# Running most of the first feed-forward's second product on scaled float16 halves

## The chip, the cores and the metric

One core of one Trainium2 chip runs the whole program. The metric is the device time of one launch in microseconds. The engines are named as the profile names them: PE (TensorE matmul), PEld (its weight loads), DVE (VectorE), ACT (ScalarE), POOL (GpSimd), SP (the queue that issues the DMAs).

## What is computed

Attention with a decay over 4 batches of 8 heads, 576 positions and a head size of 64, then two feed-forward layers over the 2304 tokens, with a model width of 512 and a hidden width of 2048.

```python
scores = scale * np.matmul(q, k.transpose(0, 1, 3, 2))
decay = cum[:, :, :, None] - cum[:, :, None, :]        # cum: running sum of log f
scores = np.where(causal, -1000000000.0, scores + decay)
attn = np.exp(scores - np.max(scores, axis=-1, keepdims=True))
attn = attn / (np.sum(attn, axis=-1, keepdims=True) + 1e-09)
x = np.matmul(attn, v)          # as 2304 x 512
h = x @ moe_w_in;   x = (h * (1.0 / (1.0 + np.exp(-h)))) @ moe_w_out
h = x @ moe2_w_in;  x = (h * np.cos(h)) @ moe2_w_out
```

All inputs are float32. A product of two matrices is made of three matmuls on two-part operands: high times high, high times low, low times high.

## The kernel before

The tokens are cut into 9 blocks of 256 (`NB`, `TB`), the hidden width into 8 pairs of 128-column chunks (`NPR`). A *step* is one layer, one block, one pair; `order` lists 72 steps of the first layer and 72 of the second. In a step the PE first makes `in` (L1086): two chunks times 4 pieces of the model width times 3 products, 24 matmuls of 128x128 by 128x256 on float16 halves, into a PSUM tile `h`. ACT and DVE then make the gated value: tanh (L1111, ACT), `d1` (L1114, DVE), `g` (copied to the high part by `copies`, L286 on ACT or L288 on DVE) and `gl` (the low part, by `rest`, L306 on DVE). Two steps later (`LAG`) the PE makes `out` (L1186 in the first layer): 24 matmuls of 128x128 by 128x256 that sum into the PSUM tiles `y` over the 8 pairs of a block. In the first layer `g` and `wo` are pairs of float32 words in the PE's rounded form (`F32R`); in the second layer (`strassen`, L989) both are float16 halves, 21 matmuls a step, and the weights come from DRAM, where the first layer's time is used to park them split (tile `w16`, store L863, load L1068).

Attention runs as 32 jobs, 16 of kind "a" and 16 of kind "b", whose units make `S` matmuls, maximum and exponential (L649 on DVE, L669 on ACT), transposes `T` (L686) and `pv` (L766). The output of attention goes to DRAM in `x_d`, is loaded as `x32`, and `split_tasks` makes the scaled float16 halves `x` of a block.

Nothing runs in the order of the code. Each piece of work is a `Task` with an engine, an estimated duration, a key, the tasks that it needs and the buffers that it takes; `Scheduler.run` plays them against its estimates, gives each free engine the ready task with the smallest key, and so writes one fixed instruction order per engine. An engine then executes its row in that order and waits where something is late. Some tasks may go to either of two engines.

```python
k_in, k_out, k_el = MK + n, MK + n + LAG[l] + 0.5, MK + n      # MK = -1000, n the step
ts = add("PE", pe, f_s, split + [masked], key=i - 10000.0, ...  # attention's S: ahead of all steps
t = add("PE", 0.1, f_sum, [t], key=key - 10000.0, acq=["s"], name="sc")   # a norm
```

So on the PE attention goes first where it is ready, and steps fill the rest; on ACT and DVE the elementwise work of the steps goes first, then attention by its position (0 to 152), then the second layer's weights (`C2K0` = 150 and up).

`scale_tasks` gives a power of two for a pair of operands: ACT squares them (L311), DVE adds (L376), the PE sums over the partitions with one matmul of one column (L380, "norm"), and DVE makes scale and inverse in four small steps (L385 to L388).

Of the kernel before, what the change touches and what calls it, by code (L numbers as in the profile page):

```python
# [23 lines left out]
TB = 256  # L24
# [19 lines left out]
W2N0, W2N1 = 16, 1.4  # L44
QA, QB = 768, 1600
# [223 lines left out]
def decay_attention_silu_cos_kernel(ctx, tc, qa, qb, f, w1i, w1o, w2i, w2o, out):  # L269
# [10 lines left out]
    w2_d = {("i", c): dr.tile([128, 2, 512], F16, name=f"w2i_d{c}") for c in range(NF)}  # L280
    w2_d.update({("o", p, k): dr.tile([128, 2, 512 if k < 3 else 256], F16, name=f"w2o_d{p}_{k}") for p in range(NPR)
# [33 lines left out]
    def sbt(tag, shape, dt=F32, name=None):  # L315
        return sb.tile(shape, dt, tag=tag, bufs=TOK[tag], name=name or tag)
# [19 lines left out]
    rg2 = sb.tile([128, NPR], F32, name="rg2")  # L336
    v2 = sb.tile([128, 2, NPR], F32, name="v2")
    vm = sb.tile([128, 4], F32, name="vm")
    ry2 = sb.tile([128, NB], F32, name="ry2")
# [28 lines left out]
    SW = lambda l, kind, p: 2 * NB + (0 if l == 1 else NPR if kind == "i" else 2 * NPR) + p  # L368
# [459 lines left out]

    w2_done = {}
# [72 lines left out]
    xready, factor, last_out = {}, {}, {}  # L902
# [32 lines left out]
    def factor_tasks(l, j, ts, key):  # L935
        k, o = SX(l, j), SW(l, "i", 0)

        def f1(p0, p1):
            def f():
                nc.vector.tensor_scalar(rg1[:, j, p0:p1], inv[:, o + p0:o + p1], inv[:, k:k + 1], 0.5, ALU.mult, ALU.mult)  # L940
            return f

        def f2():
            nc.vector.tensor_scalar(ru2[:, 0, j], inv[:, o:o + NPR], inv[:, k:k + 1], 1.0, ALU.mult, ALU.mult)
            nc.vector.tensor_scalar(ru2[:, 1, j], scl[:, o:o + NPR], scl[:, k:k + 1], 2.0 ** 100, ALU.mult, ALU.min)
            nc.vector.tensor_scalar(ru2[:, 1, j], ru2[:, 1, j], RND, None, ALU.mult)
            nc.vector.tensor_scalar(ry2[:, j:j + 1], inv[:, k:k + 1], vm[:, 1:2], 2.0 ** 16, ALU.mult, ALU.mult)
        if l == 2:
            t = add("DVE", 0.4, f2, [ts, factors2], key=key, name="sc")
            return [t] * NPR  # L950
        wts = [wready[1, "i", 2 * p][0] for p in range(NPR)]
        if j < 2:
            return [add("DVE", 0.1, f1(p, p + 1), [ts, wts[p]], key=key, name="sc") for p in range(NPR)]
        t = add("DVE", 0.1, f1(0, NPR), [ts] + wts, key=key, name="sc")
        return [t] * NPR
# [88 lines left out]
    for l, j, p in order:  # L1044
# [59 lines left out]
        if l == 1:  # L1104
# [11 lines left out]
            def half(i, s=(l, j, p)):  # L1116
                if s not in g_t:
                    g_t[s] = sbt("g", [128, 2, 2 * TB], F32R)
                return g_t[s][:, i]

# [3 lines left out]
            t3 = add(**copies(lambda half=half: half(0), src, 512, ("ACT", "DVE"), half_r), deps=[t2], key=k_el, acq=["g"],  # L1124
                     name="g")
            t4 = add(**rest(lambda half=half: half(1), src, half_r, lambda half=half: half(0).bitcast(F32), 512),
# [44 lines left out]
        prev = None  # L1171
        wdeps = [t for i in range(2) for t in wready[l, "o", 2 * p + i]]
        ytag = "s" if (l, j) == (1, 1) else "y"
        for t in range(2):
            for i in range(2):
# [23 lines left out]
                prev = add("PE", c_pe(1536, TB), f, [prev] if prev else [t3, t4, last_out.get((l, j))] + wdeps, key=k_out, acq=acq, rel=rel, name="out")  # L1199
        last_out[l, j] = prev  # L1200
        if p == NPR - 1:
            x2done.setdefault(j, [])
            for t in range(2):
                def ev(l=l, j=j, t=t, cell=cell):
                    cell["o", t] = sbt("s2", [128, 512], name="yo")
                    nc.scalar.activation(cell["o", t], y_t[l, j][t], AF.Copy)
# [3 lines left out]
                t0 = add("ACT", 0.49, ev, [prev], key=k_el, acq=["s2"], rel=[ytag], name="ev")  # L1210
# [51 lines left out]
```

## Time and profile before

| | us |
|---|---|
| median of 3 runs (982.35 to 983.75) | 983.35 |
| the profiled execution's own time | 983.18 |
| its span, first to last instruction | 981.3 |
| PE busy in the span | 955.5 |
| PEld busy | 826.4 |
| DVE busy | 757.2 |
| ACT busy | 628.0 |
| POOL busy | 123.2 |

The span is what the trace holds; 1.9 us of the profiled execution lie around it. Busy time of an engine is the time in which at least one of its instructions runs. Instructions overlap on an engine, so the length of one is more than its share of the busy time, and matmul ends are modelled: what a stream of matmuls costs is read from the starts of the groups. The timeline gives groups in order of time: start, length, engine, line, operation, operands and count, and in brackets the idle time before it.

### The profile page before, as it was taken

What the parts mean: (1) busy time and instruction counts of PE and PEld (TensorE: products, weight loads), DVE (VectorE), ACT (ScalarE), POOL (GpSimd) and SP (SyncE); (2) the same over time, 40 slices, a digit from 0 to 9 for tenths busy, and PEclk for the clock granted to TensorE, in tenths of its full rate; (3) what the DMA queues carried; (4) which work ended last, traced back from release to release, by engine and by line L of the source; (5) the groups of instructions that cost most, each with busy time, mean ns of one, the idle gap of its engine ahead of it and who ended that gap; (6) DMA issues with size and microseconds to landing.
All of it is one profiled execution on the core that took longest, in us unless ns stands there. A gap on an engine that the chain in (4) does not pass through costs nothing.

```text
span 981.3 us, 20944 instructions
## 1 busy us (share of the span) xinstructions
PE 955.5 (97%) x8223; PEld 826.4 (84%) x8223; DVE 757.2 (77%) x1792; ACT 628.0 (64%) x1219; POOL 123.2 (13%) x157
## 2 busy tenths in 40 slices
PE   7996899999999999999999999999999999999997
PEld 4475688887888878889999999988888888888886
DVE  4999976677879888858778742678888888878875
ACT  6896866577776768745455432676766766766663
POOL 4865320011111121200000000000000000000000
PEclk9998899999999999999999999999999999999999
DMA  8575234435566575334433338500010001000000
GB/s 305 182 267 195 92 108 154 157 118 177 174 208 186 181 224 189 102 115 146 167 125 125 108 128 255 193 23 23 23 44 23 23 23 44 1 23 1 23 22 22
DMA packets 55906, 115.27 MB, mean 117 GB/s; under 512 B 8128, under 2 KB 18368, under 8 KB 55808
## 3 DMA queue, kind: packets, MB, share of 16 engines
q1 hardware_dynamic: 55808, 113.94, 35.0%
q8 instruction: 64, 1.05, 0.4%
q14 instruction: 34, 0.28, 0.1%
HBM read 89.20 MB, written 24.72 MB: 116 GB/s over the span
## 4 chain that ended last, share of the span: by engine, by line
PE 89%; DVE 7%; issue 1%; ACT 1%; POOL 1%; POOLq 0%; DVEq 0%; ACTq 0%
PE h L1086 37%; PE y L1186 20%; PE y L989 17%; PE pv L766 4%; PE tt L686 4%; PE st L645 3%; DVE rw L438 2%; DVE w L442 1%; DVE wi L306 1%; PE st L638 1%; PE dp L584 1%; PE st L624 1%; PE st L623 1%; DVE e L649 1%; DVE wo L300 1%
## 5 line engine op out<-in xcount | busy, mean ns | idle before, releaser
L1086 PE MATMUL h<-x,wi 128*128 128x256 f16 x3456 | 412.2, 274 | 3.1 <-ACT wi L286 1.7
L1086 PEld LDWEIGHTS <-wi 128*128 128x128 f16 x3456 | 330.0, 98 | 52.7 <-issue 6.1
L1186 PE MATMUL y<-g,wo 128*128 128x256 f32 x1728 | 238.2, 290 | 4.4 <-ACT g L286 3.6
L1186 PEld LDWEIGHTS y<-g,wo 128*128 128x128 f32 x1728 | 216.4, 192 | 11.9 <-issue 6.1
L989 PE MATMUL y<-wo,g 128*128 128x256 f16 x1512 | 176.3, 273 | 0.0
L989 PEld LDWEIGHTS <-g 128*128 128x128 f16 x1512 | 148.0, 98 | 17.1
L669 ACT ACTIVATE e<-e,su 128x128 f32<-128x128 f32 (+4 forms) x144 | 82.9, 577 | 22.5 <-DVE su L649 20.8
L1135 ACT ACTIVATE t<-h,ru 128x512 f32<-128x512 f32 x72 | 49.4, 686 | 67.3 <-PE h L1086 67.1
L1111 ACT ACTIVATE t<-h,rg 128x512 f32<-128x512 f32 x72 | 49.3, 685 | 64.1 <-PE h L1086 62.7
L1158 DVE TENSOR_TENSOR g<-t,g 128x896 f16<-128x896 f32 x72 | 78.4, 1089 | 8.7 <-ACT g L1155 5.2
L649 DVE CUSTOM_DVE_ANT_0 e<-st,dk 128x256 f32<-128x256 f32 (+3 forms) x144 | 64.1, 478 | 23.8 <-PE st L645 13.4
L288 POOL TENSOR_SCALAR e<-e,su 128x128 f32<-128x128 f32 (+4 forms) x68 | 50.7, 751 | 247.5 <-DVE su L676 135.4
L1145 DVE SCALAR_TENSOR_TENSOR t<-h,rg,t 128x512 f32<-128x512 f32 x72 | 53.9, 749 | 31.8 <-ACT t L1142 31.8
L306 DVE SCALAR_TENSOR_TENSOR g<-t,rg,g 128x512 fp32r<-128x512 f32 x72 | 55.3, 769 | 28.8 <-ACT g L286 28.2
L1141 ACT ACTIVATE t<-t,ru 128x512 f32<-128x512 f32 x72 | 51.7, 718 | 39.9 <-DVE t L1138 39.9
L1114 DVE SCALAR_TENSOR_TENSOR t<-t,h 128x512 f32<-128x512 f32 x72 | 49.2, 683 | 35.0 <-ACT t L1111 34.5
L1155 ACT ACTIVATE g<-t 128x896 f16<-128x896 f32 x72 | 67.5, 938 | 5.0 <-DVE t L1151 5.0
L286 ACT ACTIVATE g<-t,rg 128x512 fp32r<-128x512 f32 x49 | 35.3, 721 | 53.3 <-PE y L1186 50.0
L1138 DVE SCALAR_TENSOR_TENSOR t<-t,ru,h 128x512 f32<-128x512 f32 x72 | 53.5, 743 | 20.4 <-ACT t L1135 19.9
L286 ACT ACTIVATE pt<-tt 128x384 f32<-128x384 f32 (+2 forms) x90 | 44.5, 518 | 23.5 <-PE tt L686 23.1
L686 PE MATMUL tt<-ident,e 128*128 128x128 f32 x384 | 55.7, 275 | 3.4 <-POOL e L288 2.8
L1142 ACT ACTIVATE t<-t,halfpi 128x512 f32<-128x512 f32 x72 | 52.0, 722 | 2.3
(128 smaller groups left out, 1146.7 us busy)
## 6 DMA issues: line engine op xcount, KB each, us to landing
rw<-w1i SPq DMA_DIRECT2D x16, 512.0 KB, 5.2
rw<-w1o SPq DMA_DIRECT2D x16, 512.0 KB, 6.8
x<-x_d SPq DMA_DIRECT2D x16, 512.0 KB, 3.9
dk<-decay_d SPq DMA_DIRECT2D x16, 512.0 KB, 4.2
raw<-w2i SPq DMA_DIRECT2D x16, 512.0 KB, 4.9
raw<-w2o SPq DMA_DIRECT2D x16, 512.0 KB, 4.4
qs<-qb SPq DMA_DIRECT2D x16, 480.0 KB, 4.6
w2o_d<-w SPq DMA_DIRECT2D x24, 256.0 KB, 2.1
```

What stands on the lines that cost most here:

```text
L286: nc.scalar.activation(dst, src, AF.Copy, scale=scale)
L306: fn=lambda: nc.vector.scalar_tensor_tensor(out(), a(), scale(), b(), ALU.mult, ALU.subtract))
L649: nc.vector.tensor_tensor_reduce(out, s, d, -0.125, first, ALU.add, ALU.min, cell["sm"][:, o:o + 1])
L669: nc.scalar.activation(x, x, AF.Exp, bias=sm[:, i:i + 1], scale=-1.0, accum_out=sm[:, 4 + i:5 + i])
L686: nc.tensor.transpose(tt[a][:, 128 * c:128 * c + 128], e[a][:, 128 * c:128 * c + 128], ident)
L989: nc.tensor.matmul(y[bank][:, 256 * half:256 * half + 256], g[:, gi, ga], w[:, wi, 256 * col:256 * col + 256], start=p == 0 and half == 0 ...
L1086: nc.tensor.matmul(h[:, i], w[:, wi, 128 * k:128 * k + 128], x[:, xi, k], start=(i == 0 and q == 0 and k == 0), stop=(i == 1 and q == 2 an ...
L1138: nc.vector.scalar_tensor_tensor(cell["t"], cell["t"], r, cell["h"], ALU.subtract, ALU.subtract)
L1145: nc.vector.scalar_tensor_tensor(cell["t"], cell["h"], r, cell["t"], ALU.mult, ALU.mult)
L1155: nc.scalar.activation(g_t[s][:, 0], cell["w"], AF.Copy)
L1158: nc.vector.tensor_tensor(g_t[s][:, 1], cell["w"], g_t[s][:, 0], ALU.subtract)
L1186: nc.tensor.matmul(y[:, e * TB:(e + 1) * TB], w[:, wi, 128 * ec:128 * ec + 128], g[:, gi, i * TB:(i + 1) * TB], start=(st and e == 0), sto ...
```

## The change

From the fourth block on (`J16` = 3, 48 of the 72 steps of the first layer) `out` multiplies float16 halves. For that the second weight matrix, which is there as two float32 parts in `wo`, is split once more: per pair a scale (`scale_tasks`, 8 of them, two squares each on ACT), per chunk the high half (`chi`, ACT or DVE), the remainder of the high part (`left`, DVE) and the low half (`low`, DVE), in a buffer `w16` of which there are two; the chunk is stored in DRAM (16 stores). When the third block has used a pair for the last time, its two chunks are loaded over the float32 parts, in the same place (16 loads). `g` and `gl` are written as float16 with a factor `rg3` that all pairs share, for which all eight scales must be there; the result is scaled back where `y` is read out (`ev`, ACT). The new weight work has keys 80 to 87, ahead of the second layer's weights and of the last jobs of attention.

```diff
+J16, C16 = 3, 80.0
...
+    w1_d = {c: dr.tile([128, 2, 512], F16, name=f"w1o_d{c}") for c in range(NF)}
...
-    SW = lambda l, kind, p: 2 * NB + (0 if l == 1 else NPR if kind == "i" else 2 * NPR) + p
+    SW = lambda l, kind, p: 2 * NB + NPR * (2 * l - 2 + (kind == "o")) + p
...
+    w1_done, sc1 = {}, []
+    for p in range(NPR):
+        k, key = SW(1, "o", p), C16 + p
+        pair = (2 * p, 2 * p + 1)
+        hi, lo = [lambda c, i=i: wo_t[c][:, i].bitcast(F32) for i in range(2)]
+        q = [add(**squares(lambda c=c, hi=hi: hi(c), 512, sq[:, c % 2, k:k + 1]), deps=wready[1, "o", c], key=key, name="sqw")
+             for c in pair]
+        ts = scale_tasks(k, q, key, 14)
+        sc1.append(ts)
+        for c in pair:
+            st = {}
+
+            def dst(i, st=st):
+                if "t" not in st:
+                    st["t"] = sbt("w16", [128, 2, 512], F16)
+                return st["t"][:, i]
+
+            def left(st=st, c=c, k=k, hi=hi):
+                st["w"] = sbt("s2", [128, 512], name="w")
+                nc.vector.scalar_tensor_tensor(st["w"], hi(c), scl[:, k:k + 1], st["t"][:, 0], ALU.mult, ALU.subtract)
+
+            def low(st=st, c=c, k=k, lo=lo):
+                nc.vector.scalar_tensor_tensor(st["t"][:, 1], lo(c), scl[:, k:k + 1], st["w"], ALU.mult, ALU.add)
+            t5 = add(**copies(lambda dst=dst: dst(0), lambda c=c, hi=hi: hi(c), 512, ("ACT", "DVE"), lambda k=k: scl[:, k:k + 1]),
+                     deps=[ts], key=key, acq=["w16"], name="chi")
+            t6 = add("DVE", c_dve(512), left, [t5], key=key, acq=["s2"], name="clo")
+            t6 = add("DVE", c_dve(512), low, [t6], key=key, rel=["s2"], name="clo")
+            w1_done[c] = add("SP", 0.46, lambda st=st, c=c: nc.sync.dma_start(w1_d[c], st["t"]), [t6], key=key, rel=["w16"],
+                             dma=c_dma(0.26), name="w2d")
+
+    def f_v1():
+        i, o = SW(1, "i", 0), SW(1, "o", 0)
+        nc.vector.tensor_tensor(v1[:, 0], scl[:, i:i + NPR], scl[:, o:o + NPR], ALU.mult)
+        nc.vector.tensor_tensor(v1[:, 1], inv[:, i:i + NPR], inv[:, o:o + NPR], ALU.mult)
+        nc.vector.tensor_reduce(vm[:, 2:3], v1[:, 0], AX.X, ALU.min)
+        nc.vector.tensor_reduce(vm[:, 3:4], v1[:, 1], AX.X, ALU.max)
+        nc.vector.tensor_scalar(rg3, v1[:, 1], vm[:, 2:3], 2.0 ** -16, ALU.mult, ALU.mult)
+    factors1 = add("DVE", 0.9, f_v1, sc1 + [wready[1, "i", 2 * p][0] for p in range(NPR)], key=-500, name="sc")
...
+        def f3():
+            nc.vector.tensor_scalar(ry1[:, j:j + 1], inv[:, k:k + 1], vm[:, 3:4], 2.0 ** 15, ALU.mult, ALU.mult)
+        if j >= J16:
+            ry_done[j] = add("DVE", 0.2, f3, [ts, factors1], key=key, name="sc")
...
                 if s not in g_t:
-                    g_t[s] = sbt("g", [128, 2, 2 * TB], F32R)
+                    g_t[s] = (sbt("g", [128, 2, 2 * TB], F32R) if s[1] < J16 else
+                              sbt("g", [128, 2, 4 * TB], F16)[:, :, 0:2 * TB])
                 return g_t[s][:, i]
+
+            def out_r(j=j, p=p, half_r=half_r):
+                return half_r() if j < J16 else rg3[:, p:p + 1]
+
+            def whole(j=j, half=half):
+                return half(0).bitcast(F32) if j < J16 else half(0)
 
             t1 = add("ACT", 0.49, a1, [prev, factor[l, j][p]], key=k_el, acq=["t"], name="tanh")
             t2 = add("DVE", 0.61, d1, [t1], key=k_el, rel=["h"], name="d1")
             src = lambda cell=cell: cell["t"]
-            t3 = add(**copies(lambda half=half: half(0), src, 512, ("ACT", "DVE"), half_r), deps=[t2], key=k_el, acq=["g"],
+            t3 = add(**copies(lambda half=half: half(0), src, 512, ("ACT", "DVE"), out_r),
+                     deps=[t2, factors1 if j >= J16 else None], key=k_el, acq=["g"],
                      name="g")
-            t4 = add(**rest(lambda half=half: half(1), src, half_r, lambda half=half: half(0).bitcast(F32), 512),
+            t4 = add(**rest(lambda half=half: half(1), src, out_r, whole, 512),
                      deps=[t3], key=k_el, rel=["t"], name="gl")
...
+        if j == J16:
+            for c in (2 * p, 2 * p + 1):
+                def load16(c=c):
+                    wo_t[c] = sb.tile([128, 2, 1024], F16, tag=f"wo{c}", bufs=1, name="wo")[:, :, 0:512]
+                    nc.sync.dma_start(wo_t[c], w1_d[c])
+                wready[1, "o", c] = [add("SP", 0.46, load16, [w1_done[c], out_done[J16 - 1, p]], key=k_in - 2, dma=c_dma(0.26),
+                                         name="w2l")]
...
-                prev = add("PE", c_pe(1536, TB), f, [prev] if prev else [t3, t4, last_out.get((l, j))] + wdeps, key=k_out, acq=acq, rel=rel, name="out")
-        last_out[l, j] = prev
+                prev = add("PE", (c_pe if j < J16 else c_pe16)(1536, TB), f, [prev] if prev else [t3, t4, last_out.get((l, j))] + wdeps, key=k_out, acq=acq, rel=rel, name="out")
+        last_out[l, j] = out_done[j, p] = prev
...
-                    nc.scalar.activation(cell["o", t], y_t[l, j][t], AF.Copy)
+                    nc.scalar.activation(cell["o", t], y_t[l, j][t], AF.Copy, scale=1.0 if j < J16 else ry1[:, j:j + 1])
...
-                t0 = add("ACT", 0.49, ev, [prev], key=k_el, acq=["s2"], rel=[ytag], name="ev")
+                t0 = add("ACT", 0.49, ev, [prev, ry_done.get(j)], key=k_el, acq=["s2"], rel=[ytag], name="ev")
```

Since the scheduler plans with the new tasks too, the rows of all engines move from the middle of the first stretch on. Two places follow.

The PE at `out` of the ninth step (`n` = 8, first or second block), before. `y` is the output, `nrm` a norm, `tt` a transpose and `pv` the last product of attention:

```order
L1186 MATMUL y<-g,wo 128x256 x6
L686 MATMUL tt<-ident,e 128x128 x6
L1186 MATMUL y<-g,wo 128x256 x6
L380 LDWEIGHTS ones_138
L380 MATMUL nrm<-sq_142,ones_138 128x1
L1186 MATMUL y<-g,wo 128x256 x6
L766 MATMUL pv<-pt,v 64x256 x2
L766 MATMUL pv<-pt,v 64x128 x2
L1186 MATMUL y<-g,wo 128x256 x6
```

and with the change (L1250 is L1186 of before, L385 is L380):

```order
L385 LDWEIGHTS ones_154
L385 MATMUL nrm<-sq_158,ones_154 128x1
L1250 MATMUL y<-g,wo 128x256 x6
L385 LDWEIGHTS ones_154
L385 MATMUL nrm<-sq_158,ones_154 128x1
L1250 MATMUL y<-g,wo 128x256 x6
L385 LDWEIGHTS ones_154
L385 MATMUL nrm<-sq_158,ones_154 128x1
L1250 MATMUL y<-g,wo 128x256 x6
```

Ten attention matmuls have left this `out`, and two more norms stand in it. Counted between the last `in` matmul of the ninth step and that of the eighteenth, attention has 168 matmuls before and 90 with the change, and there are 3 and 10 norms.

DVE around `d1` of the sixteenth step (L1114; the `x` rows are the split of a block's input, `qk` and `su` belong to attention), before:

```order
L288 TENSOR_SCALAR g<-t,rg_145 128x512
L940 TENSOR_SCALAR rg_145<-inv 128x8
L306 SCALAR_TENSOR_TENSOR g<-t,rg_145,g 128x512
L288 TENSOR_SCALAR pt<-tt 64x2x64
L300 TENSOR_TENSOR qk<-qs,qk 128x960
L288 TENSOR_SCALAR x<-x_2278,scl 128x512
L1114 SCALAR_TENSOR_TENSOR t<-t,h 128x512
L306 SCALAR_TENSOR_TENSOR x<-x_2278,scl,x 128x512 x2
L649 ISA e,su<-st,dk 128x384
L649 ISA su 128x1
L649 ISA e,su<-st,dk 128x384
L649 ISA su 128x1
```

and with the change (L1163 is L1114, L308 is L306, L290 is L288, L381 is L376, L393 is L388; L853 is `left`, L856 `low`):

```order
L381 SCALAR_TENSOR_TENSOR sq_158<-sq 128x1
L308 SCALAR_TENSOR_TENSOR g<-t,rg_161,g 128x512
L856 SCALAR_TENSOR_TENSOR w_2343<-wo,scl,w 128x512
L390 TENSOR_SCALAR inv<-nrm 128x1
L391 TENSOR_SCALAR inv<-inv 128x1
L392 TENSOR_SCALAR scl<-inv 128x1
L393 TENSOR_SCALAR inv<-scl 128x1
L853 SCALAR_TENSOR_TENSOR w<-wo,scl,w_2365 128x512
L290 TENSOR_SCALAR x<-x_2271,scl 128x512
L985 TENSOR_SCALAR rg_161<-inv 128x8
L1163 SCALAR_TENSOR_TENSOR t<-t,h 128x512
L308 SCALAR_TENSOR_TENSOR x<-x_2271,scl,x 128x512 x2
```

`left` and `low` of the new weight halves stand between the gate's own rows. The `x` rows at this place split the input of the fourth block before and of the third block with the change, which is the one that the next step on the PE reads. Between `d1` of the ninth and of the eighteenth step the change has 14 `left`, 13 `low`, 5 `chi` and 8 scales more on DVE, and fewer attention rows (30 maxima of L649 before, 20 with the change, and shorter ones).

## Rows read from the trace of the kernel before

**Rows 1.** The page, first part: busy time of the engines over the span.

```profile
PE 955.5 (97%) x8223; PEld 826.4 (84%) x8223; DVE 757.2 (77%) x1792; ACT 628.0 (64%) x1219; POOL 123.2 (13%) x157
```

**Rows 2.** Busy time in stretches; columns named in the first line.

```profile
core 0: us, PE busy (x) PEld busy (x) DVE busy (x) ACT busy (x) POOL busy (x), PEclk, DMA share, GB/s
25.00:50.00 25.00, 23.41 (x149) 11.99 (x146) 24.69 (x70) 20.61 (x62) 21.14 (x23) 1.00 0.58 186
50.00:75.00 25.00, 23.98 (x203) 18.72 (x202) 24.34 (x62) 22.56 (x61) 16.28 (x21) 1.00 0.74 268
75.00:100.00 25.00, 16.62 (x112) 13.75 (x111) 24.40 (x54) 15.26 (x37) 12.19 (x13) 0.81 0.50 179
100.00:129.60 29.60, 27.57 (x225) 22.01 (x225) 27.21 (x79) 24.70 (x67) 12.18 (x16) 0.93 0.28 90
129.60:163.30 33.70, 33.70 (x292) 28.19 (x291) 23.04 (x80) 20.16 (x58) 2.31 (x5) 1.00 0.40 120
163.30:205.30 42.00, 42.00 (x361) 36.42 (x360) 26.64 (x70) 25.59 (x54) 1.90 (x3) 1.00 0.46 152
205.30:260.70 55.40, 55.40 (x471) 45.44 (x471) 43.29 (x123) 39.57 (x87) 11.00 (x15) 1.00 0.57 179
480.00:560.00 80.00, 80.00 (x702) 75.52 (x702) 63.55 (x144) 39.52 (x75) 3.72 (x5) 1.00 0.38 129
```

**Rows 3.** Timeline of ACT: tanh of the ninth and the eighteenth step.

```profile
129.62 0.69 ACT L1111 ACTIVATE t<-h,rg 128x512 f32<-128x512 f32 x1
...
205.34 0.69 ACT L1111 ACTIVATE t<-h,rg 128x512 f32<-128x512 f32 x1 [0.73 <-PE h L1086]
```

**Rows 4.** Timeline of PE in the first layer: one step, and a norm.

```profile
546.21 3.12 PE L1186 MATMUL y<-g,wo 128*128 128x256 f32 x24
549.17 2.79 PE L1086 MATMUL h<-x,wi 128*128 128x256 f16 x24
551.72 3.11 PE L1186 MATMUL y<-g,wo 128*128 128x256 f32 x24
...
578.88 0.17 PE L380 MATMUL nrm<-sq,ones 128*128 128x1 bf16 x1
578.91 0.60 PE L1086 MATMUL h<-x,wi 128*128 128x256 f16 x4
```

**Rows 5.** Timeline of PE in the second layer: one step.

```profile
705.40 2.78 PE L1086 MATMUL h<-x,wi 128*128 128x256 f16 x24
708.02 2.46 PE L989 MATMUL y<-wo,g 128*128 128x256 f16 x21
710.32 2.78 PE L1086 MATMUL h<-x,wi 128*128 128x256 f16 x24
```

**Rows 6.** Groups by line and shape: count, busy, mean ns, idle before.

```profile
L1186 PE MATMUL y<-g,wo 128*128 128x256 f32 x1728 | 238.2, 290 | 4.4 <-ACT g L286 3.6 <-DVE g L306 0.8
...
L306 DVE SCALAR_TENSOR_TENSOR w<-w,sq,w 128x512 f16<-128x512 f32 x16 | 13.4, 855 | 0.2
...
L376 DVE SCALAR_TENSOR_TENSOR sq<-sq 128x1 bf16<-128x1 f32 x42 | 7.9, 189 | 1.3 <-ACT junk L311 1.3
...
L385 DVE TENSOR_SCALAR inv<-nrm 128x1 int32<-128x1 int32 x42 | 6.4, 151 | 8.6 <-PE nrm L380 8.4
```

**Rows 7.** Timeline of DVE late in the first layer: float16 low parts.

```profile
561.34 0.74 DVE L306 SCALAR_TENSOR_TENSOR w<-w,scl,w 128x512 f16<-128x512 f32 x1
562.00 0.74 DVE L306 SCALAR_TENSOR_TENSOR g<-t,rg,g 128x512 fp32r<-128x512 f32 x1
```

**Rows 8.** Waits of the DMA queue: us in total, times, longest.

```profile
SPq L863 <- DVE w L306: 107.6, 36, 11.5
SPq L539 <- PE pv L766: 67.8, 16, 9.9
```

**Rows 9.** DMA issues: count, size, median us from issue to landing.

```profile
w2i_d<-w SPq DMA_DIRECT2D x16, 256.0 KB, 2.2
wi<-w2i_d SPq DMA_DIRECT2D x16, 256.0 KB, 3.2
```

More of the change, by code (lines that the diff above doesn't have):

```diff
@@ L336, in decay_attention_silu_cos_kernel @@
     rg2 = sb.tile([128, NPR], F32, name="rg2")
+    rg3 = sb.tile([128, NPR], F32, name="rg3")
+    ry1 = sb.tile([128, NB], F32, name="ry1")
     v2 = sb.tile([128, 2, NPR], F32, name="v2")
     vm = sb.tile([128, 4], F32, name="vm")
+    v1 = sb.tile([128, 2, NPR], F32, name="v1")
     ry2 = sb.tile([128, NB], F32, name="ry2")
@@ L901, in decay_attention_silu_cos_kernel @@
     nstep = {s: n for n, s in enumerate(order)}
-    xready, factor, last_out = {}, {}, {}
+    xready, factor, last_out, ry_done, out_done = {}, {}, {}, {}, {}
     x2done = {}
```

## The prediction

> **What bounds the kernel now.** I read the page's busy times first: the PE is busy for 955.5 of 981.3 us, every other engine much less [rows 1]. An average says little over stages, so the table of stretches comes next [rows 2]. Up to 129.6 us DVE is the full engine (24.3 to 24.7 of each 25 us, then 27.2 of 29.6) and the PE waits for it, worst between 75 and 100 us, where it runs 16.6 of 25 us at a granted clock of 0.81. From 129.6 us on the PE is busy in every microsecond of every stretch and DVE is not: 23.0 + 26.6 = 49.7 us of the 75.7 from 129.6 to 205.3, 43.3 of 55.4 after that, 63.6 of 80 late in the layer. So from 130 us on a microsecond of PE work saved is a microsecond of the run, as long as DVE and ACT still deliver in time, and a microsecond of DVE work costs nothing, as long as it fits into DVE's gaps. The question is whether the change, which takes work off the PE and puts work on DVE, leaves the PE the bound everywhere.
>
> What a matmul costs is read from starts, not from busy time: by its mean an `out` matmul takes 290 ns [rows 6], but they overlap. In the first layer a step of 24 `out` and 24 `in` takes 551.72 - 546.21 = 5.51 us [rows 4]. In the second layer a step of 24 `in` and 21 `out`, all in float16, takes 710.32 - 705.40 = 4.92 us [rows 5], 0.1093 us a matmul.
>
> **The change, part by part.**
>
> *Float16 `out`.* 48 steps keep their count of matmuls. At 0.1093 us each a step of 48 takes 5.25 us in place of 5.51, so 0.26 us less, and 48 x 0.26 = **12.6 us less**. No row shows this very matmul, but the `in` of the same step has its shape, its types and its kind of operands (weights still, tokens moving), so I take its price. Upper end: the group of 24 alone takes 549.17 - 546.21 = 2.96 us [rows 4], 0.123 each, which would give (0.123 - 0.109) x 1152 = 16 us; part of that is the next group's start, which the modelled ends blur. Lower end: nothing, the first rival.
>
> *Eight norms on the PE.* The next matmul starts 0.03 us after a norm does [rows 4]: 8 x 0.03, **0.3 us more**. That is the price if its input is there. A norm stands ahead of everything else in the order and the PE waits at it if DVE's small sum is late; that belongs to the stretch below.
>
> *Weights split again.* On DVE 16 `left` and 16 `low`: the nearest rows are the float16 low parts, 0.855 us long on average in one group [rows 6], but 0.66 us from start to start where DVE is not disturbed [rows 7]; I take 0.66, so 21 us in all. Eight scales: five small instructions, 7.9 us for 42 of the first and 6.4 us for 42 of each of the other four [rows 6], (7.9 + 4 x 6.4) / 42 = 0.8 us, 6.4 us in all. With some `chi` and the five of the shared factor some 31 us. DVE has the room over the layer: 12 of the 55 us after 205.3 and 16 of the 80 late in the layer are idle [rows 2]. But the order puts nearly all of it between the ninth and the twentieth step, with ACT's 16 squares mostly ahead of it and ACT's 11 `chi` in it.
>
> *The stretch from the ninth to the eighteenth step.* Before, it lasts from 129.6 to 205.3 us [rows 3], 75.7 us, all PE: nine steps at 5.51 are 49.6, and 168 attention matmuls the other 26.1. With the change 90 remain there, so 26.1 x 90/168 = 14.0, and the PE needs 63.6 us. The rest of attention moves behind, where the same matmuls cost the same. DVE had 49.7 us of work. It gains 27 low parts at 0.66 (17.8), five `chi` at about 0.4 (2.0), eight scales (6.4), and some 2 us for two more rows of first-layer weights and the factor, 28 in all; it loses ten maxima, all of the long ones of 320 to 512 columns among them, with the normalisations and evictions that go with them, and the split of one block's input, about 15 us when each row that the order drops is counted at its mean. That makes 63 us. So in this stretch **DVE needs as long as the PE**, where it needed two thirds. In the parts of the trace where DVE is the bound it is busy for 92 to 98% of the time [rows 2], so 63 us of work take 64 to 68.5. `d1` may come late by about the length of an `out` (2.9 us) before the PE notices, since `out` runs two steps behind. I take **3 us of PE waiting**, with 0 and 9 as ends: 0 if the two steps of lead and the shift of work cover it, 9 if DVE's waits for ACT, for `w16` and for the norms add up. The first place to look is the start of the third block: its input split now ends one DVE row after `d1` of the step before, where before the change that place held the split of the fourth block, a whole block ahead.
>
> *The opening.* Up to the ninth step the order holds 23 attention matmuls fewer (6 `S`, 9 `T`, 8 `pv`) and the DVE rows that go with them, some 4 us, while DVE is full. Part of that is PE work that only moves behind. I take **1 us less**; ends 4 less and 2 more, since any new order of a DVE-bound opening can lose as well.
>
> *What I cost at nothing.* 16 stores and 16 loads of 256 KB: 2.2 and 3.2 us to landing [rows 9]; a pair is loaded after the third block's `out` of it and used eight steps later, over 40 us. The cover is gone only if SP stands still that long. `g` and `gl` in float16 read and write the same number of elements; the wait for the shared factor is over at the thirteenth step and first asked at the twenty-fifth. The read-out of `y` gets a factor on ACT, 12 times, on an engine with a third of its time free. Attention ends some six steps later, at the forty-fourth step; its last output is wanted at the sixty-fifth. Layer two is not touched.
>
> Sum: -12.6 + 0.3 - 1 + 3 = -10.3. The profiled execution took 983.2 us in its own time, 0.2 less than the median of the runs. So **973 us**; the ends of the terms give 967 to 980.
>
> **The rivals.**
>
> *No gain in the matmul.* The change only pays if the PE takes float16 faster than the rounded float32. If the count of columns alone set the pace, 12.6 falls away and 983.2 + 0.3 - 1 + 3 = 985.5 us comes out, slower. Against it: one step of mixed types takes 5.51 us and 48 float16 matmuls at the second layer's pace 5.25, on one clock [rows 2, 4, 5]. The Trainium skill, "TensorE: Matmul & The Clock Gate", section "Back-to-back issue gap", gives a gap by columns alone, 262 cycles or 109.2 ns for 256 columns, and no word on the type. The trace agrees with it for float16 and not for the rounded float32, so it bears this rival out only if something else slows the mixed step. 4 in 100.
>
> *DVE stays short.* If DVE's fullness doesn't end at the eighteenth step but lasts while the last `low` and the delayed attention share it with the second layer's weights, the PE's losses go to the far end and beyond, 9 to 13 us in place of 3: 979 to 983, likeliest 980. For it: the estimates in the scheduler are shorter than the rows, and attention's delayed rows come on top of a DVE that had 43.3 of 55.4 us filled [rows 2]. Against: after that DVE has 12 us of gaps in 55. 17 in 100.
>
> *The store blocks the buffer.* Only two `w16` exist. A `chi` waits in ACT's or DVE's row for the store of the chunk two before, and that store waits in SP's row behind attention's loads, which themselves wait: for `pv` 16 times, 67.8 us in all, 4.2 each, longest 9.9 [rows 8]. While `chi` waits, tanh and `g` stand behind it. It decides from three such waits on (3 x 4.2 = 12.6 eats the gain); with four it is 973 + 17 = 990 us, slower. Against: stores of the second layer's weights have the same place in SP's row, wait 107.6 us in all for DVE [rows 8], and the PE doesn't idle. 5 in 100.
>
> *The opening does better.* If the new order frees the PE's wait between 75 and 100 us (8.4 us lost there [rows 2]) by 5 to 8 us: 965 to 969. 8 in 100.
>
> **How the numbers follow.** The forecast has 66 in 100. The measurement of this kernel can tell about 0.2%, 2 us, from no change. Faster by over that (below 981.4): forecast 66, better opening 8, 12 of the 17 where DVE stays short: 0.86. Within it: the other 5: 0.05. Slower: 4 + 5: 0.09. The range from 966 to 981.5 holds nearly all of the forecast, most of the case where DVE stays short and half of the better opening; what it leaves out is some 2 in 10.
>
> **What would show it.** In the timeline of the changed kernel 24 `out` from the fourth block on should be 2.6 us from start to start and a step 5.25. In the table of stretches DVE should be over 90% busy from the ninth to the eighteenth step, and the idle time before the PE's `in`, `out` and norm rows there should sum to about 3 us, the largest piece ahead of the third block's first `in` or at a norm. After the forty-fourth step the PE should not wait. I am wrong if the step stays at 5.5 us; if the PE idles over 9 us behind 130 us; or if SP's waits ahead of the new stores show up as waits of `chi`.

## The result, and the profile after

| | before | changed |
|---|---|---|
| median | 983.12 us (982.35 to 983.75) | 965.67 us (965.27 to 966.1) |
| runs | 4 | 4 |
| ratio, 95% interval | | 0.9823 [0.9806, 0.984] |
| span of the profiled execution | 981.3 us | 964.0 us |

The kernel is 17.5 us faster. The forecast was 973.0, so the gain was foretold at 10 and is 7 more; the time lies 0.3 us below the range. The lines below answer to those shown of before. The page's first line [rows 1]:

```profile
PE 940.2 (98%) x8233; PEld 800.7 (83%) x8233; DVE 778.3 (81%) x1872; ACT 646.2 (67%) x1266; POOL 129.1 (13%) x161
```

PE lost 15.3 us of busy time and its span 17.3: the other 2 us are waits. The stretches [rows 2], with the columns of that table. 122.0 and 187.8 us are the ninth and the eighteenth step, where before had 129.6 and 205.3; the stretch from 122.0 overlaps the one ahead of it by 3 us:

```profile
25.00:50.00 25.00, 23.33 (x148) 12.11 (x147) 24.54 (x60) 21.24 (x64) 20.42 (x22) 1.00 0.54 184
50.00:75.00 25.00, 23.22 (x191) 17.43 (x189) 24.72 (x66) 22.08 (x64) 17.04 (x22) 1.00 0.65 229
75.00:100.00 25.00, 18.05 (x125) 15.33 (x126) 24.69 (x57) 21.80 (x54) 16.52 (x16) 0.86 0.64 234
100.00:125.00 25.00, 24.79 (x221) 21.81 (x219) 24.69 (x70) 22.96 (x60) 7.11 (x11) 1.00 0.17 56
122.00:148.30 26.30, 26.30 (x234) 23.20 (x232) 24.92 (x92) 16.08 (x37) 1.49 (x2) 1.00 0.24 81
148.30:187.80 39.50, 39.50 (x344) 33.85 (x345) 34.29 (x97) 26.26 (x71) 5.54 (x8) 1.00 0.55 184
187.80:235.80 48.00, 48.00 (x414) 41.12 (x413) 43.72 (x122) 36.18 (x81) 8.53 (x11) 1.00 0.76 250
480.00:560.00 80.00, 80.00 (x739) 71.56 (x738) 62.88 (x148) 40.74 (x75) 4.29 (x6) 1.00 0.38 135
```

Three things are to be seen. Late in the layer the PE starts 739 matmuls in 80 us where it started 702 [rows 2]. Between the ninth and the eighteenth step DVE is busy for 24.92 + 34.29 = 59.2 of 65.8 us, and the PE for all 65.8: DVE is nearly as full as foretold (90%; 95 in the first part and 87 in the second), yet the PE does not wait. And between 100 and 125 us the PE is busy for 24.79 us at full clock; the same stretch of before:

```profile
100.00:125.00 25.00, 23.03 (x186) 18.48 (x186) 24.06 (x73) 21.45 (x61) 8.93 (x12) 0.91 0.33 106
```

Tanh of the ninth and the eighteenth step on ACT's timeline [rows 3]:

```profile
121.95 0.68 ACT L1160 ACTIVATE t<-h,rg 128x512 f32<-128x512 f32 x1
...
187.76 0.69 ACT L1160 ACTIVATE t<-h,rg 128x512 f32<-128x512 f32 x1
```

A first-layer step on PE's timeline [rows 4]; `out` is L1250 and `in` L1135 now:

```profile
512.02 2.78 PE L1250 MATMUL y<-g,wo 128*128 128x256 f16 x24
514.64 2.78 PE L1135 MATMUL h<-x,wi 128*128 128x256 f16 x24
517.26 2.78 PE L1250 MATMUL y<-g,wo 128*128 128x256 f16 x24
```

24 float16 `out` take 2.62 us from start to start and a step 5.24, where a step took 5.51: 0.27 us less. The groups by form of `out`, of `left` and `low`, of the sum for a norm and of a `chi` on DVE [rows 6]:

```profile
L1250 PE MATMUL y<-g,wo 128*128 128x256 f16 x1152 | 136.8, 273 | 0.0
L1250 PE MATMUL y<-g,wo 128*128 128x256 f32 x576 | 83.2, 295 | 1.4 <-ACT g L288 0.8 <-DVE g L308 0.5
...
L856 DVE SCALAR_TENSOR_TENSOR w<-wo,scl,w 128x512 f16<-128x512 f32 x16 | 12.1, 768 | 0.1
...
L853 DVE SCALAR_TENSOR_TENSOR w<-wo,scl,w 128x512 f32<-128x512 f32 x16 | 11.8, 745 | 0.0
L381 DVE SCALAR_TENSOR_TENSOR sq<-sq 128x1 bf16<-128x1 f32 x50 | 9.4, 201 | 3.0 <-ACT junk L313 3.0
...
L290 DVE TENSOR_SCALAR w<-wo,scl 128x512 f16<-128x512 f32 x5 | 2.4, 480 | 0.0
```

No float16 `out` waited for anything, and neither did a `chi` (0.0 here, and 0.1 for the 11 on ACT). The new stores' wait in SP's row [rows 8], and the new DMAs [rows 9]:

```profile
SPq L861 <- DVE w L856: 34.3, 13, 6.5
```

```profile
w1o_d<-w SPq DMA_DIRECT2D x16, 256.0 KB, 2.2
wo<-w1o_d SPq DMA_DIRECT2D x16, 256.0 KB, 4.0
```

So the transfers cost nothing on the path, as foretold. Where the 7 us of extra gain come from is the question of the runs.

### The profile page after: what moved, and what is told of

The parts are those of the page before. It is cut to its first block, busy times and chain, and to the rows that moved or that the text cites. A ratio compares the mean times of both kernels' runs of the same rounds, so it can differ in the third digit from the quotient of the medians.

```text
span 964.0 us, 21153 instructions
## 1 busy us (share of the span) xinstructions
PE 940.2 (98%) x8233; PEld 800.7 (83%) x8233; DVE 778.3 (81%) x1872; ACT 646.2 (67%) x1266; POOL 129.1 (13%) x161
## 4 chain that ended last, share of the span: by engine, by line
PE 89%; DVE 8%; issue 1%; POOL 1%; ACT 1%; DMA 0%; POOLq 0%; DVEq 0%; SPq 0%; ACTq 0%
PE h L1135 37%; PE y L1250 19%; PE y L1038 17%; PE pv L771 5%; PE tt L691 4%; PE st L650 3%; DVE w L447 1%; DVE rw L443 1%; PE st L643 1%; DVE wi L308 1%; DVE wo L302 1%; DVE e L654 1%; PE dp L589 1%; PE st L629 1%; PE st L628 1%
## 5 line engine op out<-in xcount | busy, mean ns | idle before, releaser
L1135 PE MATMUL h<-x,wi 128*128 128x256 f16 x3456 | 409.4, 273 | 0.8 <-DVE wi L308 0.5
L1135 PEld LDWEIGHTS <-wi 128*128 128x128 f16 x3456 | 333.1, 98 | 46.8 <-issue 7.1
L1250 PE MATMUL y<-g,wo 128*128 128x256 f16 (+1 forms) x1728 | 220.1, 280 | 1.4 <-ACT g L288 0.8
L1250 PEld LDWEIGHTS <-wo 128*128 128x128 f16 x1152 | 110.7, 98 | 15.3 <-issue 2.3
L290 POOL TENSOR_SCALAR e<-e,su 128x128 f32<-128x128 f32 (+4 forms) x67 | 50.7, 762 | 266.2 <-DVE su L681 147.6
L1250 PEld LDWEIGHTS y<-g,wo 128*128 128x128 f32 x576 | 74.2, 195 | 5.9 <-issue 2.4
L308 DVE SCALAR_TENSOR_TENSOR g<-t,rg,g 128x512 f16<-128x512 f32 (+1 forms) x72 | 55.7, 773 | 22.8 <-ACT g L288 22.2
L288 ACT ACTIVATE g<-t,rg 128x512 f16<-128x512 f32 (+1 forms) x49 | 35.3, 720 | 50.4 <-PE y L1250 47.3
L1163 DVE SCALAR_TENSOR_TENSOR t<-t,h 128x512 f32<-128x512 f32 x72 | 49.0, 681 | 20.3 <-ACT t L1160 20.1
L288 ACT ACTIVATE pt<-tt 128x384 f32<-128x384 f32 (+2 forms) x94 | 46.0, 515 | 20.5 <-PE tt L691 19.2
```

The lines of the kernel that those rows point to most:

```text
L288: nc.scalar.activation(dst, src, AF.Copy, scale=scale)
L308: fn=lambda: nc.vector.scalar_tensor_tensor(out(), a(), scale(), b(), ALU.mult, ALU.subtract))
L1135: nc.tensor.matmul(h[:, i], w[:, wi, 128 * k:128 * k + 128], x[:, xi, k], start=(i == 0 and q == 0 and k == 0), stop=(i == 1 and q == 2 an ...
L1250: nc.tensor.matmul(y[:, e * TB:(e + 1) * TB], w[:, wi, 128 * ec:128 * ec + 128], g[:, gi, i * TB:(i + 1) * TB], start=(st and e == 0), sto ...
```

## The experiments

My first theory, from the two traces: about 13 us come from the float16 `out`, 4 from the opening, whose order the scheduler writes anew, and the preparation costs little. The first four kernels take the change apart.

### All of the preparation, nothing used

```diff
-J16, C16 = 3, 80.0
+J16, C16 = 9, 80.0
```

> The whole preparation (squares, scales, split, 16 stores, shared factor) with J16 = 9, so that no block ever uses it and every out stays in rounded float32; no loads back. The order of the opening is word for word that of the changed kernel up to the 22nd step. Theory A (13 us of the gain are the float16 out, 4 to 4.5 us are the opening, which goes faster only because the order there differs): 983.1 - 4.4 + 0.3 for the norms = 979, and the idle and slow-clock time ahead of 125 us as in the changed kernel. Rival B (all of the gain belongs to float16, the opening is a side effect of something else): 983 to 984. Rival C (the new work on DVE does cost, 3 us or more as I forecast, and float16 gives 16): 982 or more with the opening as in the changed kernel.

980.69 us (979.32 to 981.6), ratio 0.9977 [0.9967, 0.9987]: 2.2 faster than before, with all the extra work in it and none of its use. That is 1.7 above theory A and 2.3 below B's lower end: something in the preparation gives more than the preparation takes.

### The use alone, in the opening's old order

```diff
-        q = [add(**squares(lambda c=c, hi=hi: hi(c), 512, sq[:, c % 2, k:k + 1]), deps=wready[1, "o", c], key=key, name="sqw")
...
+            w1_done[c] = add("SP", 0.46, lambda c=c: nc.sync.dma_start(w1_d[c], wi_t[c]), wready[1, "i", c], key=key,
...
+            held.append(w1_done[c])
...
+        if (l, n) == (1, 8):
+            for t in held:
+                sd.needs(t, [prev])
```

> Float16 out from the fourth block on without the preparation: no squares, no scales, no split; the 16 stores copy the first matrix's float16 halves as a stand-in of the same shape, the loads are as in the change, g and gl are float16 with the old factors. It multiplies by the wrong weights, so that the second product of the first layer isn't the reference's from the fourth block on. The stores are held until the in of the ninth step, and the order up to there is that of the kernel before. Theory A: the opening as before, 48 steps cheaper by 0.26 to 0.27 us, 983.1 - 12.9 = 970.2. Rival B: 965.7 to 967 (all of the 17 us are float16).

968.0 us (967.51 to 968.6), ratio 0.9847 [0.9832, 0.9861]: 14.9 us less than before (982.93 beside it): more than theory A's 12.9, less than B's 16 to 17.

### The change, with its preparation held until the ninth step

```diff
         q = [add(**squares(lambda c=c, hi=hi: hi(c), 512, sq[:, c % 2, k:k + 1]), deps=wready[1, "o", c], key=key, name="sqw")
              for c in pair]
+        held += q
...
+        if (l, n) == (1, 8):
+            for t in held:
+                sd.needs(t, [prev])
```

> The whole change, but the squares wait for the in of the ninth step, so that no preparation lies in the opening and the order up to the ninth step is that of the kernel before. Theory A: the opening's 4.4 us are gone, 970 to 971, with PE idle after 130 us under 1 us. Rival B: 966. Rival D (the preparation, now squeezed into fewer steps, makes DVE the bound from the ninth step on, my forecast's 3 us and more): 973 or more, with PE idle of 3 us or more after 130 us.

969.8 us (968.49 to 970.3), ratio 0.9863 [0.9848, 0.9877]. It differs from the use alone by the real preparation, 1.8 us. From the change it differs by 4.1 us, by the order of the opening and by where behind the ninth step the preparation lies. That is theory A; the PE is idle for 0.9 us in one place at 277 us and not between 150 and 250. DVE's busy time by the pages is 755.9 us with the use alone and 780.9 here: 25 us of new DVE work cost 1.8.

### Twice the remainders and low halves

```diff
-                nc.vector.scalar_tensor_tensor(st["w"], hi(c), scl[:, k:k + 1], st["t"][:, 0], ALU.mult, ALU.subtract)
+                for _ in range(2):
+                    nc.vector.scalar_tensor_tensor(st["w"], hi(c), scl[:, k:k + 1], st["t"][:, 0], ALU.mult, ALU.subtract)
...
-                nc.vector.scalar_tensor_tensor(st["t"][:, 1], lo(c), scl[:, k:k + 1], st["w"], ALU.mult, ALU.add)
+                for _ in range(2):
+                    nc.vector.scalar_tensor_tensor(st["t"][:, 1], lo(c), scl[:, k:k + 1], st["w"], ALU.mult, ALU.add)
```

> The change with each left and low issued twice in a row, 32 more two-input DVE instructions of 0.66 us, 21 us of DVE work between the 9th and the 20th step, in an order that is otherwise the same on every engine. It measures how far DVE was from being the bound. Theory A with room (DVE was 88 to 95% busy in the changed kernel there, the two steps of lag absorb the rest): the first 5 or so us are free, the rest is waited for, 965.7 + 8 to 16 = 974 to 982. Rival E (DVE has real room, waits are absorbed as attention shifts): under 970. If DVE had been the bound already: 965.7 + 21 = 987.

986.79 us (985.09 to 987.41), ratio 1.0032 [1.0019, 1.0046]: 21.1 us more than the change, as much as the extra DVE work (32 at 0.66; by the pages DVE's busy time grows by 23.2). It is what the expectation gave for a DVE that had been the bound already; theory A's 974 to 982 falls. The stretches behind 125 us:

```profile
125.00:150.00 25.00, 20.05 (x173) 17.69 (x172) 23.64 (x72) 9.76 (x19) 0.00 (x0) 1.00 0.25 77
150.00:175.00 25.00, 23.92 (x192) 19.40 (x192) 23.18 (x69) 16.62 (x46) 2.96 (x4) 0.93 0.44 140
175.00:200.00 25.00, 21.28 (x161) 17.01 (x161) 22.72 (x58) 10.81 (x31) 1.83 (x4) 0.93 0.41 140
200.00:225.00 25.00, 21.22 (x161) 17.43 (x162) 24.51 (x49) 15.37 (x34) 2.94 (x4) 0.93 0.61 223
```

The PE waits 4.95 + 1.08 + 3.72 + 3.78 = 13.5 us here, where it waits for nothing with the change, and runs at a granted clock of 0.93 in three of the four stretches. By the trace DVE ended some 9 us of these waits, POOL and ACT the rest.

### Half of that: the remainders alone twice

Edit: of the two loops above only the first.

> The change with left alone issued twice: 16 more DVE instructions of 0.66 us, 10.5 us, half of what e4_double added (there 21 us of DVE work cost 21.1 us). Theory G (the preparation of the change fills DVE to the brim between the ninth and the eighteenth step, so any more counts in full): 10 us more, 975 to 977. Rival H (some room is left, and the cost sets in above it): under 5 us more, below 971, with the PE's idle time behind 125 us below 3 us.

972.55 us (972.14 to 972.89), ratio 0.9895 [0.9878, 0.9911]: 6.9 us more than the change for 10.5 us of DVE work (12.1 by the pages' busy time), between the two expectations. The same stretches:

```profile
125.00:150.00 25.00, 22.80 (x200) 19.74 (x199) 23.61 (x85) 12.56 (x28) 0.00 (x0) 1.00 0.24 80
150.00:175.00 25.00, 24.24 (x204) 20.00 (x202) 22.87 (x57) 15.84 (x43) 2.95 (x4) 1.00 0.62 196
175.00:200.00 25.00, 24.00 (x203) 19.85 (x203) 24.54 (x59) 14.79 (x37) 2.60 (x5) 1.00 0.46 166
200.00:225.00 25.00, 24.26 (x203) 20.26 (x203) 23.86 (x70) 19.22 (x43) 5.06 (x7) 1.00 0.75 238
```

4.7 us of PE waits, the clock still full. So, as an estimate, the change left DVE some 10.5 - 6.9 = 3.6 us of room in that stretch (5.2 by the busy time); what goes beyond counts in full. The second 10.5 us cost 14.2, more than their own length: only there the clock falls too.

### Only the squares

The next pair asks what turned the opening. First the kernel before with the 16 squares on ACT and nothing behind them.

```diff
+    for p in range(NPR):
+        k, key = SW(1, "o", p), C16 + p
...
+        q = [add(**squares(lambda c=c, hi=hi: hi(c), 512, sq[:, c % 2, k:k + 1]), deps=wready[1, "o", c], key=key, name="sqw")
+             for c in pair]
```

> The kernel before with only the 16 squares of the new weight work added (on ACT, nothing reads what they sum): no scales, no halves, no stores, float32 out everywhere. The squares alone are enough to turn the scheduler's row: up to the tenth step the PE's order is that of the change, 90 attention matmuls fewer than before being no part of it, but 6 S, 9 T and 8 pv. Theory A (4 of the 17 us come from the new order of the opening, and from nothing else in the change): 979 us, 978 to 980; tanh of the ninth step at about 122 us instead of 129.6, and no other gain behind it. Theory B (the whole gain is float16): 983 to 984. If the squares cost their own time on a full ACT: over 984.

978.63 us (977.99 to 979.37), ratio 0.9955 [0.9941, 0.9968]: 4.2 us faster by work that nobody reads. By the traces the PE's matmuls are in the order of the change up to 125.8 us. Tanh of the ninth and of the 49th step, behind the last of attention:

```profile
121.71 0.68 ACT L1128 ACTIVATE t<-h,rg 128x512 f32<-128x512 f32 x1
...
481.33 0.69 ACT L1128 ACTIVATE t<-h,rg 128x512 f32<-128x512 f32 x1 [1.97 <-PE h L1103]
```

Before had them at 129.62 [rows 3] and 485.49: the ninth comes 7.9 us earlier, and when the attention that was put off has been made up, 4.2 us are left. The stretches to hold against those of before (16.62 at clock 0.81 in [rows 2], then 23.03 at 0.91 above):

```profile
75.00:100.00 25.00, 18.41 (x128) 15.54 (x128) 24.69 (x57) 21.37 (x52) 12.56 (x14) 0.80 0.63 221
100.00:125.00 25.00, 24.52 (x218) 21.58 (x216) 24.69 (x70) 23.36 (x60) 6.73 (x11) 1.00 0.18 58
```

### Attention put back by another knob

The kernel before, without any of the new work, and the change, each with later attention jobs further back:

```diff
-GAP4, GAP8 = 8, 16
+GAP4, GAP8 = 16, 16
```

> The kernel before with one number changed, none of the new work: GAP4 = 16 instead of 8, which puts the later attention jobs further back. Before the ninth step's end the PE's order then holds 12 S, 9 T and 8 pv fewer. Theory A1 (any order with that much attention moved behind the ninth step frees the PE in the DVE-bound opening): 978 to 980, PE idle before 125 us below 11, granted clock between 75 and 125 us higher. Theory A2 (the gain hangs on the particular order the squares bring about): 982 to 985, with idle time of the PE that only moves to another place.

> The change with GAP4 = 16 instead of 8: attention up to the ninth step as little as in the change, but more of it between the ninth and the eighteenth step (31 S, 19 T and 14 pv more), beside the preparation, and other rows in the opening. Theory A1 (the opening gains by attention put back, whatever puts it back): within 1.5 of the change, 964 to 967. Theory A2 (the gain hangs on the particular order): 968 to 971, the opening's 4 us lost again. If DVE, which has no room left in that stretch, now falls short: PE idle behind 125 us of 2 us or more.

The kernel before becomes slower, 989.21 us (988.51 to 990.22), ratio 1.0065 [1.0052, 1.0077]; the change comes to 977.69 (976.14 to 978.27), ratio 0.9942 [0.993, 0.9955], 12 us worse than without this edit. Both are slower than any of the theories had them. Both have as little attention ahead of the ninth step as the change or less, so that is not what helps: A1 falls, and what is left of A2 is that the particular order decides, by more than I thought. The opening of before with the edit, then of the change with it, and the PE's wait in the latter:

```profile
75.00:100.00 25.00, 18.57 (x147) 14.06 (x148) 24.62 (x53) 18.59 (x50) 20.11 (x23) 0.91 0.71 246
100.00:125.00 25.00, 21.06 (x150) 18.48 (x147) 23.67 (x61) 16.42 (x36) 0.76 (x1) 0.84 0.07 22
```

```profile
75.00:100.00 25.00, 18.77 (x148) 14.03 (x147) 24.72 (x52) 20.03 (x55) 18.87 (x21) 0.98 0.64 210
100.00:125.00 25.00, 17.03 (x101) 12.80 (x101) 24.35 (x85) 20.69 (x54) 4.37 (x3) 0.68 0.16 57
```

```profile
104.67 1.05 PE L1250 MATMUL y<-g,wo 128*128 128x256 f32 x4
111.44 0.16 PE L385 MATMUL nrm<-sq,ones 128*128 128x1 bf16 x1 [5.72 <-DVE su L654]
```

In the kernel before the wait has only moved, from 75 to 100 us to 100 to 125: it is 10.4 us in these 50 with the edit and without. In the change it grows from 7.2 to 14.2: behind its `out` a norm stands in the PE's row for 5.72 us.

### Float16 only where no attention is left

As the use alone, with `J16` = 6: 24 steps.

```diff
-J16, C16 = 3, 80.0
+J16, C16 = 6, 80.0
```

> As e2_use_only (float16 out with stand-in weights, nothing split, the opening in the order of before), but from the seventh block on: 24 steps instead of 48, all of them behind the last of attention. Theory C (a step alone gains 24 x 11.2 ns = 0.27 us by the pace; a step broken up by attention and norms gains more, since each return to the rounded float32 costs about 0.1 us that a return to float16 does not): 24 x 0.27 = 6.5 us less than before, 976.4 us, so 8.4 of the 15 us of e2_use_only belong to its first 24 steps. Rival E (every step gains the same, 15/48 = 0.31 us): 975.4 us. Rival F (the pure steps gain 0.26 as forecast and part of the 15 us is the order of the stretch behind the ninth step, which this kernel has as e2_use_only): 974 to 975.

974.98 us (974.19 to 975.47), ratio 0.9919 [0.9905, 0.9934], 7.9 us less than before. Theory C, that a step among attention gains more, falls: it asked for 8.4 us between this kernel and the use alone, and there are 7.0 for 24 steps, 0.29 each. The median lies at F's upper end, 0.4 us below E, which is no more than the runs spread; the trace decides. Tanh of the 49th and of the 72nd step, in before, then here:

```profile
485.49 0.69 ACT L1111 ACTIVATE t<-h,rg 128x512 f32<-128x512 f32 x1 [1.91 <-PE h L1086]
...
612.58 0.69 ACT L1111 ACTIVATE t<-h,rg 128x512 f32<-128x512 f32 x1 [1.98 <-PE h L1086]
```

```profile
484.21 0.69 ACT L1132 ACTIVATE t<-h,rg 128x512 f32<-128x512 f32 x1 [0.75 <-PE h L1104]
...
605.54 0.69 ACT L1132 ACTIVATE t<-h,rg 128x512 f32<-128x512 f32 x1 [1.96 <-PE h L1104]
```

At the 49th step, ahead of the first float16 `out`, 1.3 us are already won; from there to the 72nd it is 127.09 - 121.33 = 5.8 us, in which some 22 `out` lie (they run two steps behind): 0.26 each. So F holds: a float16 step gains 0.26 to 0.29, 13 us in 48, and one or two of the 15 come from the order of attention behind the ninth step, which is written anew as well. What in that order gives them was not tried, and the 1.3 us rest on one profiled execution of each kernel.

### One block earlier, and two

The change with `J16` = 2 and with `J16` = 1.

```diff
-J16, C16 = 3, 80.0
+J16, C16 = 2, 80.0
```

> The change with J16 = 2: float16 out from the third block on, 56 steps instead of 48, the same preparation. Theory C (the gain per step is 24 x 11 ns by the pace plus about 0.1 us for each time the PE comes back to the rounded float32 from something else): eight steps among attention at 0.27 to 0.36 us, 2.2 to 2.9 less than the change, 962.8 to 963.5. Rival D (the halves are not ready at the nineteenth step, where they would now be asked for, since DVE is full until there): the PE waits ahead of the third block's out, 966 to 970.

963.82 us (962.76 to 964.36), ratio 0.9804 [0.9791, 0.9818]. The eight steps give 1.9 us, 0.23 each, a little under C's lower end. The interval overlaps with that of the change; the runs themselves do not (965.27 is the change's fastest). It is the fastest kernel of this study.

```diff
-J16, C16 = 3, 80.0
+J16, C16 = 1, 80.0
```

> The change with J16 = 1: float16 out from the second block on, 64 steps. The halves are now asked for at the eleventh step, so the scheduler pulls the preparation forward: 9 of the 16 low parts stand before the eleventh d1 on DVE (5 before the twelfth with J16 = 2), in the stretch where DVE is already full. Theory G (DVE is short there, and DVE work counts in full once its few us of room are used): the eight more float16 steps give 2.2 us, the crowded stretch takes 5 to 15: 967 to 977, with the PE's idle time between 100 and 200 us over 5 us. Rival C (the gain goes on with each block, since the PE has attention to fill in with): 961.5 to 962.

976.74 us (976.51 to 978.11), ratio 0.994 [0.9926, 0.9953], within theory G's 967 to 977: the gain ends where the halves are asked for in a stretch in which DVE is full. The place is the 25 us ahead of the ninth step's tanh, which comes at 147.83 us instead of 121.06 with `J16` = 2:

```profile
125.00:150.00 25.00, 19.30 (x117) 12.46 (x114) 23.96 (x106) 18.55 (x55) 3.38 (x5) 0.74 0.65 206
```

117 matmuls at a clock of 0.74, where the change starts 234 in the 26.3 us from 122.0 on. The PE waits 5.7 us here, 4.4 of them ended by DVE and 1.3 by ACT. But this order also puts more attention there: 229 of its matmuls between the last `in` of the ninth and of the eighteenth step, where the change has 90 and `J16` = 2 has 80. How much of the loss is the crowded DVE and how much the attention beside it was not taken apart.

## Why the prediction was wrong

**The step that failed** is the size of the opening: "I take 1 us less; ends 4 less and 2 more". It gave 4.1 us (held preparation against the change) and 4.2 (squares alone against before). I had priced it by the work that leaves it, some 4 us of DVE rows of which "part of that is PE work that only moves behind". The work that moves was right: the ninth tanh comes 129.62 - 121.95 = 7.7 us earlier, and 23 attention matmuls at the 0.155 us of my own term (26.1 / 168) are 3.6 of these; 4.1 are left, which is the gain. But it is not the price of moved work. The PE's waits from 25 to 125 us shrink by 2.4 us (100 less the four busy times: 13.0 before, 10.6 after), which leaves, as an estimate, 1.7 for the clock. It rises from 0.91 to 1.00 between 100 and 125 us, in the change and with the squares alone. Between 75 and 100 us it shows 0.81 before, 0.86 in the change and 0.80 with the squares alone, whose order there is the change's, so that figure tells nothing. What the rows could tell was how much lay there to be won: between 75 and 125 us the PE waited 8.4 + 2.0 = 10.4 us and lost at most (0.19 + 0.09) x 25 = 7 us to the clock, an estimate as if it were busy throughout. A new order can also lose: the two runs with the other knob lost 6 and 12, not all of it in the opening. That one wins much more than 4 no run shows. So the term lay at its own fast end, and I had taken it near its middle. The rival "the opening does better" had the time, 965 to 969, at 8 in 100; it looked for 5 to 8 us of freed wait between 75 and 100 us, where 1.4 us of it are, with 1.8 behind 100. That its time came true is in part luck: the opening gave 3 us more than forecast, the other terms the rest.

The range was also added up too narrowly. "967" takes the opening at 4 less and the full stretch at nothing, but leaves float16 at its middle. With that term's own upper end of 16 the fast ends give 983.2 - 16 + 0.3 - 4 = 963.5, and the slow ends give 983.2 - 12.6 + 0.3 + 2 + 9 = 981.9, not 980.

**The other terms.** Each term was measured by two pairs of runs, which share no kernel between the two. The first figures are the steps from before over the use alone and the held preparation to the change, the second those from before over the squares alone and the preparation alone; so each three add up to the whole by construction, and the finding is that the two ways agree within 0.3 us:

| term | forecast | measured |
|---|---|---|
| float16 `out`, 48 steps | -12.6 | -14.9 (use alone against before), -15.0 (change against preparation alone) |
| preparation: norms, DVE, PE waits | +0.3 + 3 | +1.8 (held against use alone), +2.1 (preparation alone against squares alone) |
| opening | -1 | -4.1, -4.2 |
| sum | -10.3 | -17.2 (means of the pairs; the medians of before and after differ by 17.5) |

*Float16 `out`.* Mechanism and price were right: 2.62 us for 24 against 2.6 foretold, a step 5.24 against 5.25. The new `out` runs at 2.62 / 24 = 109.2 ns a matmul, the rounded float32 at (5.51 - 2.62) / 24 = 120 ns. The Trainium skill ("TensorE: Matmul & The Clock Gate", section "Back-to-back issue gap") gives 262 cycles, or 109.2 ns, for 256 columns, as the gap of an isolated matmul, and is silent on the rounded float32. The trace agrees with it for the new `out`. The term was 2.4 us short since 48 x 0.27 is 13.0, and the rest I put down to the new order of attention, for which I had no term (1.3 us of it are seen at the 49th step above).

*The full stretch.* DVE got nearly as full as I counted: 59.2 us busy where I had 63, with 25 us of new work where I had 31. The PE needed 65.8 us where I had 63.6, so DVE had more room than the sum allowed; what came late did not reach the PE. "3 us of PE waiting" was nothing that the stretch's row shows; the runs with doubled work place the edge some 3.6 us of DVE work further on. Where the 1.8 to 2.1 us lie that the preparation costs after all was not followed. So the reason was right, and the change stops just short of where it would have applied. The place that I named first, the third block's input, did not wait.

*The rivals.* "No gain in the matmul" fell with the 2.62 us. "DVE stays short" did not happen, but the doubled work brought it about, and `J16` = 1 something like it. "The store blocks the buffer": the stores waited 13 times, 34.3 us in all, longest 6.5, and no `chi` waited for one.

All three terms missed to the same side, by 3.1, 1.4 and 2.4 us. As I read it, I had taken the middle of ends that are not independent of each other, since one new order decides the waits of the opening, of the full stretch and of attention behind it; no run shows that they go together.

## What to carry to other kernels

Where a scheduler writes the order, adding any work writes it anew, and in a stretch that is bound by waits this alone was worth several microseconds of either sign here (4 less, 6 and 12 more): give it a term of its own around zero, with ends from the waits that lie in the stretch, and measure it by adding the work without its use. Price added work on a nearly full engine by the room in the stretch where the order puts it: up to the room it costs next to nothing, beyond it everything and more. When the use of a cheaper form is moved earlier, try each place: here one block more paid 1.9 us, and the next, whose preparation falls into the stretch that is already full, cost 13.

## What the runs showed of the hardware

A wait of the PE can cost more than its length. With the doubled remainders and low halves the PE does the same matmuls as in the change, but its busy time by the pages is 946.4 us against 940.2: 6.2 us on top of the waits, in stretches with a granted clock of 0.93. By the clock alone it would be at most 0.07 x 75 = 5.3 us, an estimate from these stretches. With half of the extra work the waits are 4.7 us in all, none of the four stretches falls below 1.00, and busy time rises by 1.8 us only. The lowest clock in the stretches shown stands beside the longest wait: 0.68 from 100 to 125 us of the change with `GAP4` = 16, where the PE stood 5.72 us ahead of a norm. But one long wait is not needed: the 0.74 of `J16` = 1 stands beside waits of 1.45 us at most, 5.7 in all.

A change of type between matmuls costs nothing by itself here. A group of 24 in float32 takes 2.96 us from its start to the next [rows 4], though 24 x 120 ns are 2.88, so I had suspected a price for each return from float16 (theory C). By the starts in the trace of before, at 41 such returns between 281 and 612 us, the first `out` starts 28 ns after the last `in` (median) and the second 202 ns after the first: 230 ns for the two, as 109 + 120 would give. The 0.08 us are a first matmul that is started early, and the step pays only the pace.
